# Native float32 second products for the first eight pairs, and a first-weights product as four side-by-side tiles that DMA spreads

## The chip, the cores and the metric

The kernel runs on one core of a Trainium2 chip. The metric is the device time of one execution in microseconds (us); lower is better. Engines work in parallel, each in its own program order: PE (matrix products; PEld is its weight loading), DVE, ACT and POOL (elementwise work), and SP, which here issues every DMA.

## The reference

```python
# x: (4, 12480, 128)   inducing: (32, 128)   w_in: (128, 2048)   w_out: (2048, 128)
def mab(q, kv):
    s = scale * (q @ kv.transpose(0, 2, 1))
    s = s - s.max(-1, keepdims=True)
    a = np.exp(s)
    a /= a.sum(-1, keepdims=True) + 1e-09
    return a @ kv
h = mab(I, x)                 # 32 induced points for each batch, over all 12480 tokens
y = mab(x, h)                 # each token attends to the 32 points
r = np.maximum(y @ w_in, 0.0)
out = (s * (r * r) + b) @ w_out
```

## The kernel before

The tokens of a batch form 26 blocks of 480 (`BLK`); four batches give 104 blocks. The 2048 hidden features form 16 chunks of 128, taken two at a time: 8 *pairs* for a block, 832 pairs in all, numbered `k`.

**The two products of a pair.** The kernel never forms `y`. It multiplies the induced points with `w_in` first (`w_unit`, tile `wst`), so that the first product of a pair is `wst` times the attention weights `a2t` of the block. Matmuls on `float32r` operands are the quick kind; on plain `float32` operands the same matmul leaves two records and takes longer. To keep accuracy with `float32r`, an operand is split in a rounded high part and the rest: `wst` holds the high part of the points' product in rows 0 to 63 and the low part in rows 64 to 127, `a2t` repeats its own high and low parts to match, and `w_out` is split in `w_hi` and `w_lo` (`split_w_out`). After the first product (`pair`, two matmuls, PSUM tile `h`, three buffers) ACT or DVE takes the relu `r`, ACT squares it in `float32r` (`square`, tile `g1`), DVE forms the exact square `g` (called the S step below, L831), and POOL or DVE subtracts the two for the rest `g2` (L845). The second product (`out_part`) is six matmuls: `w_lo` and `w_hi` on `g1`, `w_hi` on `g2`.

**Work beside the pairs.** For each batch there are, beside the pairs of the batch before: `scores` (seven groups of up to four blocks), `top`, `values` (seven groups, each with two halves of the keys' tile `xn`, L633), `points` (the induced points, `hT`), `w_unit` (four chunks of 512 features, L560, each with an ACT cast L562 and a DVE subtraction L564), and `attend` (seven groups, L681 and the DVE steps L687 to L712). `spread` sends an attend's high and low parts (tile `hl`, two buffers) to `a2t` (three buffers) by four SP DMAs for a block (L774). `scores`, `attend` and `values` use PE on tiles of 32 columns, four side by side.

**The opening.** Batch 0 has nothing to hide behind: its phase 1 runs first (`p1_unit`, `turn_x`), then `h_unit`, `h_out` (tile `hT`), four chunks of `w_unit`, `attend_first` (the first block alone, `a2t` by PE and ACT), and only then pairs. The weights arrive as 64-bit floats and `narrow` makes them `float32` by integer steps on DVE (L291 to L307), ACT and POOL (L312), chunk by chunk; `w_out`'s chunks are then split, and summed for the bias (`w_sum`, L329; `bias_unit`). `keep_warm` issues idle matmuls until the first `a2t` is there.

**What sets the order.** Class `Plan` is a planner that runs while the program is built. Each step names an engine, an expected duration, events to wait for and an urgency; the planner takes steps by expected start plus `WEIGHT` (0.0272 us) times urgency, lowest first, and so writes out a fixed order for every engine. Constants such as `FIRST`, `FIRST_FRONT`, `W_IN_U`, `W_OUT_U`, `SPREAD` are urgencies; `ATTEND_AT`, `W_AT` and others are block numbers at which work beside the pairs is placed. `front_work` strings the work beside a block into one chain. The planner also decides for each pair whether POOL or DVE does the subtraction (`kind`).

Of the kernel before, what the change touches and what calls it, by code (L numbers as in the profile page):

```python
# [19 lines left out]
P = 128  # L20
# [29 lines left out]
SPREAD = -50.0  # L50
FIRST_FRONT = -120.0
W_IN_U = -190.0
W_OUT_U = -100.0
W_URGENCY = (1.5, 20.0, 21.0, 22.0)

# [9 lines left out]
H_AT = 20  # L65
W_AT = (20, 21, 21, 21)
NEXT_AT = 23
# [76 lines left out]
def tile_attn_relu2(ctx: ExitStack, tc: tile.TileContext, xT, xN, indT, w_in, w_out, s_rep, b_rep, outT):  # L144
# [123 lines left out]
    def load_weight(gate, name, c):  # L268
        turn, free = ring("g1", 4)
        yield "SP", 0.05, free, *gate  # L270
        sl = slice(c * WC, (c + 1) * WC)
        src, dst = (w_in, w_in_sb) if name == "w_in" else (
            w_out.rearrange("p f d -> p (f d)"), w_out_raw.rearrange("p f d -> p (f d)")
        )
        raw = ew.tile([P, WC, 2], I32, name="g1", bufs=4)
        nc.sync.dma_start(out=raw.rearrange("p n w -> p (n w)"), in_=src[:, sl].bitcast(I32))
        raws[name, c] = raw, turn
        plan.events["raw", name, c] = landing(1.46)
        plan.spawn(narrow((name, c), dst[:, sl], ("raw", name, c)), W_IN_U if name == "w_in" else W_OUT_U)
        if name == "w_out":  # L280
            plan.spawn(split_w_out(c), W_OUT_U)


    def narrow(name, dst, *waits):
        raw, turn = raws.pop(name)
        hi, lo = raw[:, :, 1], raw[:, :, 0].bitcast(U32)
        e_turn, e_free = ring("g", 4)
        m_turn, m_free = ring("g2", 8)
        yield "DVE", 0.36, e_free, *waits
        e = ew.tile([P, WC], I32, name="g", bufs=4)  # L290
        nc.vector.tensor_scalar(  # L291
            out=e, in0=hi, scalar1=20, scalar2=0x7FF, op0=ALU.logical_shift_right, op1=ALU.bitwise_and
        )
        yield "DVE", 0.36, m_free
        m = ew.tile([P, WC], I32, name="g2", bufs=8)
        nc.vector.tensor_scalar(out=m, in0=hi, scalar1=0xFFFFF, scalar2=None, op0=ALU.bitwise_and)
        yield "DVE", 0.36
        nc.vector.tensor_scalar(out=e, in0=e, scalar1=896.0, scalar2=1151.0, op0=ALU.max, op1=ALU.min)
        yield "ACT", 0.5
        nc.scalar.activation(out=dst, in_=m, func=AF.Copy, scale=2.0**-20, bias=1.0)  # L300
        plan.set(("g2", m_turn))
        yield "ACT", 0.5
        nc.scalar.activation(out=e, in_=e, func=AF.Copy, scale=2.0**23, bias=-896 * 2.0**23)
        yield "DVE", 0.6
        nc.vector.scalar_tensor_tensor(out=dst, in0=lo, scalar=2.0**-52, in1=dst, op0=ALU.mult, op1=ALU.add)
        yield "DVE", 0.6
        nc.vector.scalar_tensor_tensor(  # L307
            out=e, in0=hi, scalar=-0x80000000, in1=e, op0=ALU.bitwise_and, op1=ALU.bitwise_or
        )
        plan.set(("g1", turn))  # L310
        yield "Pool", 1.4
        nc.gpsimd.tensor_tensor(out=dst, in0=dst, in1=e.bitcast(F32), op=ALU.mult)  # L312
        plan.set(("g", e_turn))
        plan.set(name)

    def split_w_out(c):
        raw = w_out_raw
        sl = slice(c * (WC // P), (c + 1) * (WC // P))
        yield "ACT", 0.6, ("w_out", c)
        nc.scalar.copy(out=w_hi[:, sl, :], in_=raw[:, sl, :])  # L320
        yield "Pool", 1.3
        nc.gpsimd.tensor_tensor(
            out=w_lo[:, sl, :], in0=raw[:, sl, :], in1=w_hi[:, sl, :].bitcast(F32), op=ALU.subtract
        )
        plan.set(("w_split", c))
        if c % 2:
            both = slice((c - 1) * (WC // P), (c + 1) * (WC // P))
            yield "DVE", 1.15, ("w_out", c - 1)
            nc.vector.reduce_sum(  # L329
                out=w_sum[:, c // 2, :], in_=raw[:, both, :].rearrange("p f d -> p d f"), axis=AX.X  # L330
            )
        plan.set(("w_sum", c))
# [217 lines left out]

    def w_unit(b, c, ps, *waits):
        d = st[b]
        lo = P // 2
        sl = slice(c * WC, (c + 1) * WC)
        yield "PE", 0.85, ("hT", b), ("w_in", c), *waits
        if c == 0:
            d["wst"] = wst_pool.tile([P, F], F32R, name="wst")
        wst = d["wst"]
        ps = ps()
        nc.tensor.matmul(ps, d["hT"], w_in_sb[:, sl], start=True, stop=True)  # L560
        yield "ACT", 0.6
        nc.scalar.copy(out=wst[:, sl], in_=ps)  # L562
        yield "DVE", 0.6
        nc.vector.tensor_sub(out=wst[lo:P, sl], in0=ps[lo:P, :], in1=wst[lo:P, sl].bitcast(F32))  # L564
        plan.set(("wst", b, c))

# [3 lines left out]
    def scores(b, g, ps, *waits):  # L570
# [40 lines left out]
    def values(b, g, ps, *waits):  # L611
# [10 lines left out]
        plan.set(("eT", "got", e_turn))  # L622
        nc.vector.transpose(out=eT[0:rows].rearrange("p n i -> p (n i)"), in_=e)
        for half in range(-(-TB // TH)):
            runs = range(half * TH, min(TB, (half + 1) * TH))
            yield "PE", 0.055 * len(runs) + 0.1, ("xn", b, g, half)
            if half == 0:
                ps = ps()
            xn, xn_turn = xn_tiles.pop((b, g, half))
            plan.set(xn_turn)  # L630
            for n in runs:
                c = n % (P // M)
                nc.tensor.matmul(  # L633
                    ps[M * c:M * (c + 1), 0:P], eT[0:rows, n], xn[0:rows, n - runs.start],
                    start=n < P // M, stop=n + P // M >= TB,
                )
        plan.set(("eT", e_turn))
# [35 lines left out]
    def attend(b, g, ps, *waits):  # L673
        nb = blocks_in(g)
        rows = M * nb
        yield "PE", 0.2 + 0.2 * nb, ("hT", b), ("x", b, g, 2), *waits
        ps = ps()
# [29 lines left out]
        yield dict(ACT=0.56, DVE=0.65), 0.0, *free  # L707
        hl = p2.tile([P, 2, BLK], F32R, name="hl")
        plan.set(("hl", "got", n))
# [9 lines left out]
    def attend_first(ps):  # L719
# [26 lines left out]
        yield dict(ACT=0.38, DVE=0.43), 0.0  # L746
        A = p2.tile([P, 2, BLK], F32R, name="hl")
        A = A.rearrange("p a t -> p (a t)")[0:T, 0:NQ * P].rearrange("p (n r s i) -> p n r s i", n=NQ, r=2, s=2)
# [17 lines left out]
    def spread(b, g, q):  # L766

        turn, free = ring_in_order("a2t", 3)
        yield "SP", 1.4, *free, ("hl", b, g)
        t = p2.tile([P, BLK], F32R, name="a2t", bufs=3)  # L770
# [21 lines left out]
    def pair(k):  # L792
# [28 lines left out]
        plan.set(("R", k))  # L821
        q["R"].append((n, plan.end))
        if len(q["R"]) == 1:
            plan.spawn(square(k - n), k + SQ, plan.end + LAT)
        yield "DVE", 1.07, S_U
        wait = max(0.0, pool_work[0] - plan.end)
        kind = "P" if wait < POOL_Q and next_free("g", 4) <= plan.start else "D"
        if kind == "P":
            g_turn, _ = ring("g", 4)
        g = hv if kind == "D" else ew.tile([P, 2, BLK], F32, name="g", bufs=4)  # L830
# [51 lines left out]
    def out_part(k, ops, us, weights, used):  # L882
# [6 lines left out]
        first = left == 2 * NPAIR  # L889
        left -= 1  # L890
        parts[blk_g] = left
# [49 lines left out]
    for b in range(B):  # L941
        at = b * NBLK
        units = [(ATTEND_AT[g - 1], attend, b, g) for g in range(1, NG)]
        if b + 1 < B:
            units += [(SCORES_AT[g], scores, b + 1, g) for g in range(NG)]
            units += [(VALUES_AT[g], values, b + 1, g) for g in range(NG)]
            units += [(TOP_AT, top, b + 1), (H_AT, points, b + 1), (NEXT_AT, attend, b + 1, 0)]
            units += [(W_AT[c], w_unit, b + 1, c) for c in range(F // WC)]
        rank = [scores, top, values, points, w_unit, attend]
# [23 lines left out]

    def w_work(c):
        t = hs[1 + c // 2]
        yield from w_unit(0, c, lambda: t[:, c % 2])
        if c % 2:
            plan.set(("h", 1 + c // 2))

# [39 lines left out]
    def after():  # L1019
        yield "SP", 0.05, *[("p1", 0, g) for g in range(NG)]  # L1020
        plan.spawn(h_unit(0, lambda: hs[2][:, 0]), FIRST)
        plan.spawn(h_out(0, lambda: hs[2][:, 1]), FIRST)
        for c in range(F // WC):
            plan.spawn(w_work(c), FIRST + W_URGENCY[c])
        plan.spawn(attend_first(lambda: bank[0]), FIRST)
# [48 lines left out]
```

## Time and profile before

| | |
|---|---|
| median of 3 runs | 1628.44 us (1628.23 to 1628.54) |
| profiled execution, time | 1628.27 us |
| profiled execution, span of the engines | 1626.2 us |
| PE busy | 1606.7 us, 99% |
| POOL busy | 1570.5 us, 97% |
| ACT busy | 1513.9 us, 93% |
| DVE busy | 1463.8 us, 90% |
| mean granted PE clock | 0.998 of full speed |

The span is the stretch from the first to the last instruction; 2.07 us of the profiled execution lie around it. Busy times are sums over each engine; matmul ends are modelled, so the starts of successive matmuls tell more than their durations. In a row of the timeline the columns are start (us from the span's start), time (us), engine, line, operation, tile written and tile read, count of merged instructions, and in brackets how long the engine had been idle and what released it. In a row of the groups, the number after the bar is the group's busy time, then the mean of one in ns, then idle time before them.

### The profile page before, as it was taken

To read this page: it belongs to the slowest core of one execution; us is meant where nothing else is said; L and a number is where in the kernel's file an instruction comes from. 1 tells how busy PE (TensorE), PEld (TensorE's weight loads), DVE (VectorE), ACT (ScalarE), POOL (GpSimd) and SP (SyncE) were. 2 spreads that over 40 slices of the span, in tenths; PEclk is the share of its full clock that TensorE was granted. 3 is DMA by queue.
4 is the path that set the end of the run, shared out by engine and by line. 5 is a ranking of instruction groups with operands and counts; after the bars stand their busy time and mean duration, and the time that the engine had idled before them with its cause. 6 is when DMAs were issued, how large, how long until landed. Compare 5 with 4: busy or idle time off the path is not lost.

```text
span 1626.2 us, 24652 instructions
## 1 busy us (share of the span) xinstructions
PE 1606.7 (99%) x8159; PEld 1300.1 (80%) x8159; DVE 1463.8 (90%) x1587; ACT 1513.9 (93%) x1771; POOL 1570.5 (97%) x715
## 2 busy tenths in 40 slices
PE   9799999999999999999999999999999999999998
PEld 6577878888887787888788787887878888888787
DVE  6999989989998998989899989989989889999897
ACT  7799999989999999899999999999999999999997
POOL 1699999999999999999999999999999999999998
PEclk9999999999999999999999999999999999999999
DMA  7132223311133222231122322322212112112100
GB/s 270 59 110 96 75 70 113 109 50 61 37 104 112 77 92 83 88 110 55 43 67 98 103 80 73 116 80 86 61 43 68 37 50 67 32 49 68 55 31 19
DMA packets 50909, 125.99 MB, mean 77 GB/s; under 512 B 10464, under 2 KB 36960, under 8 KB 50784
## 3 DMA queue, kind: packets, MB, share of 16 engines
q1 hardware_dynamic: 50784, 124.43, 23.9%
q8 instruction: 66, 1.08, 0.3%
q14 instruction: 59, 0.48, 0.1%
HBM read 73.52 MB, written 25.56 MB: 61 GB/s over the span
## 4 chain that ended last, share of the span: by engine, by line
PE 91%; POOL 3%; DVE 2%; ACT 2%; issue 2%; DMA 0%; POOLq 0%; DVEq 0%; ACTq 0%
PE x L893 63%; PE h L803 21%; POOL g L845 3%; PE x L633 1%; PE x L681 1%; PE x L590 1%; ACT r L818 1%; PE h L404 1%; PE x L560 1%; DVE g L831 1%; ACT g L868 1%; PE x L429 0%; PE x L458 0%; DVE w_sum L329 0%; DMA xt<-in_xT_dram 0%
## 5 line engine op out<-in xcount | busy, mean ns | idle before, releaser
L845 POOL TENSOR_TENSOR g<-g,g 128x960 fp32r<-128x960 f32 x696 | 1553.5, 2289 | 4.0 <-DVE g L831 2.9
L893 PE MATMUL x<-g,w_hi 128*128 128x480 f32 x3328 | 1058.6, 382 | 2.1 <-POOL g L845 2.1
L831 DVE SCALAR_TENSOR_TENSOR g<-h,r 128x960 f32<-128x960 f32 x696 | 784.7, 1148 | 67.1 <-ACT r L818 49.8
L868 ACT ACTIVATE g<-r 128x960 fp32r<-128x960 f32 (+1 forms) x807 | 802.8, 1029 | 18.2 <-DVE r L820 5.6
L893 PEld LDWEIGHTS x<-g,w_hi 128*128 128x128 f32 x3328 | 620.8, 188 | 126.4 <-POOL g L845 16.2
L818 ACT ACTIVATE r<-h 128x960 f32<-128x960 f32 x659 | 625.6, 968 | 53.5 <-PE h L803 42.5
L893 PE MATMUL x<-g,w_lo 128*128 128x480 f32 x1664 | 636.1, 382 | 6.5 <-ACT g L868 6.5
L803 PE MATMUL h<-a2t,wst 128*128 128x480 f32 x1664 | 506.0, 385 | 1.8 <-DVE g L831 1.0
L803 PEld LDWEIGHTS h<-a2t,wst 128*128 128x128 f32 x1664 | 305.8, 188 | 81.8 <-issue 23.9
L893 PEld LDWEIGHTS x<-g,w_lo 128*128 128x128 f32 x1664 | 313.1, 188 | 60.5 <-issue 11.4
L820 DVE TENSOR_SCALAR r<-h 128x960 f32<-128x960 f32 x173 | 199.2, 1152 | 18.9 <-PE h L803 15.5
L845 DVE TENSOR_TENSOR g<-h,g 128x960 fp32r<-128x960 f32 x136 | 156.7, 1152 | 7.8 <-ACT g L868 2.1
L831 DVE SCALAR_TENSOR_TENSOR h<-h,r 128x960 f32<-128x960 f32 x136 | 157.5, 1158 | 5.5 <-ACT r L818 4.8
L901 ACT ACTIVATE ob<-x,bias,s_sb 128x480 f32<-128x480 f32 x103 | 77.0, 747 | 12.5 <-PE x L893 11.7
L312 POOL TENSOR_TENSOR w_in_sb<-w_in_sb,g 128x512 f32<-128x512 f32 x4 | 5.4, 1342 | 28.7 <-DVE g L307 28.7
L681 PE MATMUL x<-xt,hT 128*32 128x480 f32 x208 | 28.3, 578 | 0.0
L633 PE MATMUL x<-xn,eT 128*32 128x128 f32 (+1 forms) x630 | 26.9, 279 | 0.0
L633 PEld LDWEIGHTS x<-xn,eT 128*32 128x32 f32 (+1 forms) x630 | 15.6, 108 | 14.1 <-issue 11.7
L687 DVE STREAM_TRANSPOSE x<-x 128x480 f32<-128x480 f32 (+1 forms) x28 | 19.4, 693 | 7.5 <-PE x L681 6.9
L712 DVE TENSOR_TENSOR hl<-x,hl 128x480 fp32r<-128x480 f32 (+1 forms) x28 | 18.4, 656 | 5.4 <-ACT hl L175 5.1
L696 DVE TENSOR_REDUCE x<-x 128x15 f32<-128x480 f32 (+1 forms) x28 | 18.5, 661 | 4.1 <-ACT x L694 3.7
L590 PE MATMUL x<-xt,ind_sb 128*32 128x480 f32 x156 | 21.2, 578 | 0.0
(150 smaller groups left out, 416.2 us busy)
## 6 DMA issues: line engine op xcount, KB each, us to landing
xt<-in_xT_dram SPq DMA_DIRECT2D x41, 960.0 KB, 4.9
out_dram<-ob SPq DMA_DIRECT2D x104, 240.0 KB, 2.0
a2t<-hl SPq DMA_DIRECT2D x412, 60.0 KB, 2.0
xn<-in_xN_dram SPq DMA_DIRECT2D x18, 512.0 KB, 3.6
xn<-in_xN_dram SPq DMA_DIRECT2D x18, 448.0 KB, 4.4
xt<-in_xT_dram SPq DMA_DIRECT2D x13, 480.0 KB, 3.8
r<-in_xT_dram SPq DMA_DIRECT2D x7, 480.0 KB, 9.2
g<-in_w_in_dram SPq DMA_DIRECT2D x4, 512.0 KB, 11.2
```

Of the source, the lines that this page charges most:

```text
L590: nc.tensor.matmul(ps[M * q:M * (q + 1), 0:BLK], ind_sb, xt[:, q], start=True, stop=True)
L633: nc.tensor.matmul(ps[M * c:M * (c + 1), 0:P], eT[0:rows, n], xn[0:rows, n - runs.start], start=n < P // M, stop=n + P // M >= TB,)
L681: nc.tensor.matmul(ps[M * q:M * (q + 1), 0:BLK], hT[:, 0:M], xt[:, q], start=True, stop=True)
L687: nc.vector.transpose(out=s, in_=s)
L803: nc.tensor.matmul(h[:, u, 0:BLK], wst[:, c * P:(c + 1) * P], A, start=True, stop=True)
L818: nc.scalar.activation(out=r, in_=hv, func=AF.Relu)
L820: nc.vector.tensor_scalar(out=r, in0=hv, scalar1=0.0, scalar2=None, op0=ALU.max)
L831: nc.vector.scalar_tensor_tensor(out=g, in0=hv, scalar=0.0, in1=r, op0=ALU.max, op1=ALU.mult)
L845: eng.tensor_tensor(out=g2, in0=g, in1=hi.bitcast(F32), op=ALU.subtract)
L868: nc.scalar.activation(out=q["g1_t"][:, sl, :], in_=q["r_t"][:, sl, :], func=AF.Square)
L893: nc.tensor.matmul(o, w, g, start=first and n == 0, stop=left == 0 and n == len(ops) - 1)
L901: nc.scalar.activation(out=ob, in_=o, func=AF.Identity, bias=bias, scale=s_sb)
```

## The change

1. For the first eight pairs (`k < NATIVE`), the second product is two plain `float32` matmuls of `w_out_raw` on the exact square `g`: no `square`, no subtraction, and no need of `w_hi` and `w_lo`. `split_w_out` and the sums get a late urgency (`SPLIT_U`, `W_SUM_U`) in place of -100.
2. `w_unit` is one step for a batch: four matmuls of 32 columns side by side into one bank, one cast and one subtraction for all (tile `hl`), and 16 SP DMAs (`spread_w`, four for a chunk) that write the high and low parts to the rows of `wst`.
3. The PE part of `values` is one step that waits for both halves of `xn`, where it was two steps.
4. The planner's durations for `narrow`, `w_sum`, `scores`, `attend` and `spread`, and the urgency `FIRST_FRONT`, have other values. `hl` grows to 2 x 512 columns.

```diff
-FIRST_FRONT = -120.0
+FIRST_FRONT = -60.0
+SPLIT_U = 5.0
+NATIVE = 8
+W_SUM_U = 6.0
-W_URGENCY = (1.5, 20.0, 21.0, 22.0)
+W_URGENCY = 1.5
-W_AT = (20, 21, 21, 21)
+W_AT = 21
...
-            plan.spawn(split_w_out(c), W_OUT_U)
+            plan.spawn(split_w_out(c), SPLIT_U)
...
-            yield "DVE", 1.15, ("w_out", c - 1)
+            yield "DVE", 1.98, ("w_out", c - 1), W_SUM_U - SPLIT_U
...
-    def w_unit(b, c, ps, *waits):
+    def w_unit(b, ps, *waits):
         d = st[b]
-        lo = P // 2
-        sl = slice(c * WC, (c + 1) * WC)
-        yield "PE", 0.85, ("hT", b), ("w_in", c), *waits
-        if c == 0:
-            d["wst"] = wst_pool.tile([P, F], F32R, name="wst")
-        wst = d["wst"]
-        ps = ps()
-        nc.tensor.matmul(ps, d["hT"], w_in_sb[:, sl], start=True, stop=True)
-        yield "ACT", 0.6
-        nc.scalar.copy(out=wst[:, sl], in_=ps)
-        yield "DVE", 0.6
-        nc.vector.tensor_sub(out=wst[lo:P, sl], in0=ps[lo:P, :], in1=wst[lo:P, sl].bitcast(F32))
-        plan.set(("wst", b, c))
+        nc_ = F // WC
+        yield "PE", 1.3, ("hT", b), *[("w_in", c) for c in range(nc_)], *waits
+        d["wst"] = wst_pool.tile([P, F], F32R, name="wst")
+        ps = ps()
+        for c in range(nc_):
+            nc.tensor.matmul(
+                ps[M * c:M * (c + 1), :], d["hT"][:, 0:M], w_in_sb[:, c * WC:(c + 1) * WC], start=True, stop=True
+            )
+        n, free = ring_in_order("hl", 2)
+        yield dict(ACT=0.59, DVE=0.7), 0.0, *free
+        hl = p2.tile([P, 2, WC], F32R, name="hl")
+        plan.set(("hl", "got", n))
+        copy(hl[:, 0], ps)
+        yield "DVE", 0.7
+        nc.vector.tensor_sub(out=hl[:, 1], in0=ps, in1=hl[:, 0].bitcast(F32))
+        left = list(range(nc_))
+        for c in range(nc_):
+            plan.spawn(spread_w(b, c, hl, n, left), SPREAD + c, plan.end + LAT)
+
+    def spread_w(b, c, hl, n, left):
+        yield "SP", 2.4
+        wst = st[b]["wst"]
+        for r in range(P // M):
+            nc.sync.dma_start(
+                out=wst[M * r:M * (r + 1), c * WC:(c + 1) * WC].bitcast(F32),
+                in_=hl[M * c:M * (c + 1), r * M // (P // 2)].bitcast(F32),
+            )
+        left.remove(c)
+        if not left:
+            plan.set(("hl", n))
+        plan.events["wst", b, c] = landing(0.8)
...
+        yield "PE", 1.25, *[("xn", b, g, half) for half in range(-(-TB // TH))]
+        ps = ps()
+        for n in range(TB):
+            c, half = n % (P // M), n // TH
+            nc.tensor.matmul(
+                ps[M * c:M * (c + 1), 0:P], eT[0:rows, n], xn_tiles[b, g, half][0][0:rows, n - half * TH],
+                start=n < P // M, stop=n + P // M >= TB,
+            )
...
+        native = k < NATIVE
...
-        q["R"].append((n, plan.end))
-        if len(q["R"]) == 1:
-            plan.spawn(square(k - n), k + SQ, plan.end + LAT)
-        yield "DVE", 1.07, S_U
+        if native:
+            g1_used(q, 2)
+            q["r_uses"] -= 1
+            kind = "N"
+            g_turn, g_free = ring("g", 4)
+            yield "DVE", 1.07, S_U, g_free
+        else:
...
+        if kind == "N":
+            ops = [(w_out_raw[:, 2 * pr + u, :], g[:, u, :]) for u in range(2)]
+            plan.spawn(out_part(k, ops, 1.6, "w_out", lambda: plan.set(("g", g_turn))), k + OUT, plan.end + LAT)
+            return
```

More of the change, by code (lines that the diff above doesn't have):

```diff
@@ L288, in narrow @@
         m_turn, m_free = ring("g2", 8)
-        yield "DVE", 0.36, e_free, *waits
+        yield "DVE", 0.45, e_free, *waits
         e = ew.tile([P, WC], I32, name="g", bufs=4)
@@ L293, in narrow @@
         )
-        yield "DVE", 0.36, m_free
+        yield "DVE", 0.45, m_free
         m = ew.tile([P, WC], I32, name="g2", bufs=8)
         nc.vector.tensor_scalar(out=m, in0=hi, scalar1=0xFFFFF, scalar2=None, op0=ALU.bitwise_and)
-        yield "DVE", 0.36
+        yield "DVE", 0.45
         nc.vector.tensor_scalar(out=e, in0=e, scalar1=896.0, scalar2=1151.0, op0=ALU.max, op1=ALU.min)
-        yield "ACT", 0.5
+        yield "ACT", 0.63
         nc.scalar.activation(out=dst, in_=m, func=AF.Copy, scale=2.0**-20, bias=1.0)
         plan.set(("g2", m_turn))
-        yield "ACT", 0.5
+        yield "ACT", 0.63
         nc.scalar.activation(out=e, in_=e, func=AF.Copy, scale=2.0**23, bias=-896 * 2.0**23)
-        yield "DVE", 0.6
+        yield "DVE", 0.72
         nc.vector.scalar_tensor_tensor(out=dst, in0=lo, scalar=2.0**-52, in1=dst, op0=ALU.mult, op1=ALU.add)
-        yield "DVE", 0.6
+        yield "DVE", 0.72
         nc.vector.scalar_tensor_tensor(
@@ L310, in narrow @@
         plan.set(("g1", turn))
-        yield "Pool", 1.4
+        yield "Pool", 1.3
         nc.gpsimd.tensor_tensor(out=dst, in0=dst, in1=e.bitcast(F32), op=ALU.mult)
@@ L549, in h_out @@
         plan.set(("hT", b))
-    def w_unit(b, c, ps, *waits):
+    def w_unit(b, ps, *waits):
         d = st[b]
-        lo = P // 2
-        sl = slice(c * WC, (c + 1) * WC)
-        yield "PE", 0.85, ("hT", b), ("w_in", c), *waits
-        if c == 0:
-            d["wst"] = wst_pool.tile([P, F], F32R, name="wst")
-        wst = d["wst"]
-        ps = ps()
-        nc.tensor.matmul(ps, d["hT"], w_in_sb[:, sl], start=True, stop=True)
-        yield "ACT", 0.6
-        nc.scalar.copy(out=wst[:, sl], in_=ps)
-        yield "DVE", 0.6
-        nc.vector.tensor_sub(out=wst[lo:P, sl], in0=ps[lo:P, :], in1=wst[lo:P, sl].bitcast(F32))
-        plan.set(("wst", b, c))
+        nc_ = F // WC
+        yield "PE", 1.3, ("hT", b), *[("w_in", c) for c in range(nc_)], *waits
+        d["wst"] = wst_pool.tile([P, F], F32R, name="wst")
+        ps = ps()
+        for c in range(nc_):
[24 more added lines that the diff above has]
+        plan.events["wst", b, c] = landing(0.8)
     def scores(b, g, ps, *waits):
@@ L585, in scores @@
         d = st[b]
-        yield "PE", 0.2 + 0.2 * nb, ("x", b, g, 1), *waits
+        yield "PE", 0.4 + 0.23 * nb, ("x", b, g, 1), *waits
         ps = ps()
@@ L623, in values @@
         nc.vector.transpose(out=eT[0:rows].rearrange("p n i -> p (n i)"), in_=e)
-        for half in range(-(-TB // TH)):
-            runs = range(half * TH, min(TB, (half + 1) * TH))
-            yield "PE", 0.055 * len(runs) + 0.1, ("xn", b, g, half)
-            if half == 0:
-                ps = ps()
[L629 to L636, printed above, removed]
+        yield "PE", 1.25, *[("xn", b, g, half) for half in range(-(-TB // TH))]
[6 more added lines that the diff above has]
+            )
+        for half in range(-(-TB // TH)):
+            plan.set(xn_tiles.pop((b, g, half))[1])
         plan.set(("eT", e_turn))
@@ L675, in attend @@
         rows = M * nb
-        yield "PE", 0.2 + 0.2 * nb, ("hT", b), ("x", b, g, 2), *waits
+        yield "PE", 0.4 + 0.23 * nb, ("hT", b), ("x", b, g, 2), *waits
         ps = ps()
@@ L707, in attend @@
         yield dict(ACT=0.56, DVE=0.65), 0.0, *free
-        hl = p2.tile([P, 2, BLK], F32R, name="hl")
+        hl = p2.tile([P, 2, WC], F32R, name="hl")[:, :, 0:BLK]
         plan.set(("hl", "got", n))
@@ L746, in attend_first @@
         yield dict(ACT=0.38, DVE=0.43), 0.0
-        A = p2.tile([P, 2, BLK], F32R, name="hl")
+        A = p2.tile([P, 2, WC], F32R, name="hl")
         A = A.rearrange("p a t -> p (a t)")[0:T, 0:NQ * P].rearrange("p (n r s i) -> p n r s i", n=NQ, r=2, s=2)
@@ L768, in spread @@
         turn, free = ring_in_order("a2t", 3)
-        yield "SP", 1.4, *free, ("hl", b, g)
+        yield "SP", 2.4, *free, ("hl", b, g)
         t = p2.tile([P, BLK], F32R, name="a2t", bufs=3)
@@ L821, in pair @@
         plan.set(("R", k))
-        q["R"].append((n, plan.end))
-        if len(q["R"]) == 1:
-            plan.spawn(square(k - n), k + SQ, plan.end + LAT)
-        yield "DVE", 1.07, S_U
[L826 to L829, printed above, removed]
+        if native:
[5 more added lines that the diff above has]
+        else:
+            q["R"].append((n, plan.end))
+            if len(q["R"]) == 1:
+                plan.spawn(square(k - n), k + SQ, plan.end + LAT)
+            yield "DVE", 1.07, S_U
+            wait = max(0.0, pool_work[0] - plan.end)
+            kind = "P" if wait < POOL_Q and next_free("g", 4) <= plan.start else "D"
+            if kind == "P":
+                g_turn, _ = ring("g", 4)
         g = hv if kind == "D" else ew.tile([P, 2, BLK], F32, name="g", bufs=4)
@@ L889, in out_part @@
         first = left == 2 * NPAIR
-        left -= 1
+        left -= 2 if weights == "w_out" else 1
         parts[blk_g] = left
@@ L947, in tile_attn_relu2 @@
             units += [(TOP_AT, top, b + 1), (H_AT, points, b + 1), (NEXT_AT, attend, b + 1, 0)]
-            units += [(W_AT[c], w_unit, b + 1, c) for c in range(F // WC)]
+            units.append((W_AT, w_unit, b + 1))
         rank = [scores, top, values, points, w_unit, attend]
@@ L972, in turn_work, with w_work @@
         yield from turn_x(g, h, lambda: hs[j % 2], ("turn", j - 2))
[L974 to L978, printed above, removed]
+    def w_work():
+        yield from w_unit(0, lambda: hs[1][:, 0])
+        plan.set(("h", 1))
+        plan.set(("h", 2))
     def opening():
@@ L1022, in after @@
         plan.spawn(h_out(0, lambda: hs[2][:, 1]), FIRST)
-        for c in range(F // WC):
-            plan.spawn(w_work(c), FIRST + W_URGENCY[c])
+        plan.spawn(w_work(), FIRST + W_URGENCY)
         plan.spawn(attend_first(lambda: bank[0]), FIRST)
```

## The prediction

> **What bounds the kernel now.** I read the page's busy times first, then a table of stretches, to see whether one engine is the bound everywhere or only on average.
>
> ```profile
> PE 1606.7 (99%) x8159; PEld 1300.1 (80%) x8159; DVE 1463.8 (90%) x1587; ACT 1513.9 (93%) x1771; POOL 1570.5 (97%) x715
> ```
>
> ```profile
> core 0: us, PE busy (x) PEld busy (x) DVE busy (x) ACT busy (x) POOL busy (x), PEclk, DMA share, GB/s
> 52.00:60.00 8.00, 1.61 (x10) 1.05 (x6) 7.41 (x13) 5.66 (x8) 2.67 (x2) 0.89 0.36 123
> ...
> 100.00:400.00 300.00, 299.76 (x1555) 242.02 (x1554) 273.82 (x293) 281.74 (x332) 299.82 (x136) 1.00 0.27 87
> ...
> 1200.00:1600.00 400.00, 398.35 (x1830) 330.90 (x1829) 367.13 (x372) 386.73 (x434) 399.66 (x180) 1.00 0.16 49
> ```
>
> From 100 to 1600 us PE has no room: 299.76 of 300 us busy, at full clock. What leaves PE there shortens the run one for one, as long as the others follow. POOL is as full, but it shares its subtraction with DVE, which is busy 91% there. Between 52 and 60 us it is different: PE stands for 6.4 of 8 us, and the clock drops. So the steady part is priced in PE time, the opening in PE's gaps.
>
> **Steady part, `w_unit`.** I looked for what one chunk costs PE, from the starts of its neighbours:
>
> ```profile
> 391.36 1.02 PE L560 MATMUL x<-w_in_sb,hT 128*128 128x512 f32 x2
> 391.79 0.19 PEld L803 LDWEIGHTS h<-a2t,wst 128*128 128x128 f32 x1 [0.24 <-PE x L893]
> 391.82 1.00 PE L803 MATMUL h<-a2t,wst 128*128 128x480 f32 x2
> 392.66 0.60 PE L893 MATMUL x<-g,w_hi 128*128 128x480 f32 x2
> ```
>
> ```profile
> 84.90 0.38 PE L893 MATMUL x<-g,w_lo 128*128 128x480 f32 x1
> 85.12 0.38 PE L893 MATMUL x<-g,w_hi 128*128 128x480 f32 x1
> 85.43 1.01 PE L590 MATMUL x<-xt,ind_sb 128*32 128x480 f32 x8
> 86.37 0.71 PE L803 MATMUL h<-a2t,wst 128*128 128x480 f32 x2
> 86.92 0.60 PE L893 MATMUL x<-g,w_hi 128*128 128x480 f32 x2
> ```
>
> Ordinary matmuls start 0.21 to 0.22 us apart, on average 0.217. From 391.36 to 392.66 lie 1.30 us; the two L803 in them take 0.43, so a chunk costs 0.87 us, four cost 3.48. The new form is like `scores`: four 32-column tiles. From 85.12 to 86.92 lie 1.80 us, less 0.217 and 0.433 for three ordinary matmuls: 1.15 us, of which 0.94 is the group itself (85.43 to 86.37). At 512 columns that is 0.94 x 512/480 + 0.21 = 1.21 us. Saving for a batch 2.27, for batches 1 to 3 **6.8 us**. The ends: 1.00 us without any switching cost (7.4 saved) and 3.48 if the tiles did not run side by side (0 saved); `scores` has the same form, so I take 1.21. ACT loses three of four casts and DVE three of four subtractions, both of which run beside PE: nothing.
>
> **Steady part, `values`.**
>
> ```profile
> 297.38 0.38 PE L893 MATMUL x<-g,w_lo 128*128 128x480 f32 x1
> 297.59 0.37 PE L893 MATMUL x<-g,w_hi 128*128 128x480 f32 x1
> 297.90 0.64 PE L633 MATMUL x<-xn,eT 128*32 128x128 f32 x16
> 298.47 0.70 PE L803 MATMUL h<-a2t,wst 128*128 128x480 f32 x2
> 299.10 0.64 PE L633 MATMUL x<-xn,eT 128*32 128x128 f32 x14
> 299.67 0.71 PE L803 MATMUL h<-a2t,wst 128*128 128x480 f32 x2
> ```
>
> Two ordinary matmuls stand between the halves and take 0.63 us (298.47 to 299.10) where they need 0.43: going out of the tiled form and into it again costs 0.20 us. Joined, that goes, once in each of 3 batches x 7 groups = 21: **4.2 us**. If the halves of some groups already touch it is less, down to 0. The one step waits for both `xn` loads, and keeps the first buffer some 1.2 us longer (0.57 + 0.63); both are fetched two blocks ahead, some 30 us (1570 us after the opening / 104 blocks is 15 each), so nothing waits.
>
> **Steady part, the 16 DMAs.** `spread_w` goes on SP, past the `a2t` spreads:
>
> ```profile
> L774 SPq DMA_DIRECT2D a2t<-hl x412: 507/582/1692, 60.5 to 1583.1; - x138
> DMA to landing us min/median/max: 1.9/2.0/5.6
> ```
>
> ```profile
> SPq L774 <- PE h L803: 42.4, 23, 10.7
> ```
>
> 16 issues take 16 x 0.582 = 9.3 us and land 2.0 us later. `wst` is wanted five blocks (some 75 us) after `W_AT`. An `a2t` spread behind them comes 9.3 us late, but spreads waited 42.4 us for L803 to give back one of three `a2t` buffers, so they run about two blocks ahead. `hl` is held for those 11 us too; the next attend but one needs it. I take 0 and bound it in a rival.
>
> **Opening.** The rows below carry this part.
>
> ```profile
> 44.22 3.68 PE L560 MATMUL h<-w_in_sb,hT 128*128 128x512 f32 x8
> 46.36 1.08 ACT L562 CAST wst<-h 128x512 fp32r<-128x512 f32 x2
> 50.73 0.56 ACT L175 CAST a2t<-x 128x480 fp32r<-128x480 f32 x1 [0.40 <-PE x L757]
> 51.10 1.01 PE L681 MATMUL x<-xt,hT 128*32 128x480 f32 x8
> 52.04 1.57 PE L803 MATMUL h<-a2t,wst 128*128 128x480 f32 x6
> 54.51 0.70 DVE L687 STREAM_TRANSPOSE x<-x 128x480 f32<-128x480 f32 x1
> 58.20 1.79 ACT L868 ACTIVATE g<-r 128x1920 fp32r<-128x1920 f32 x1
> 59.19 0.70 DVE L705 STREAM_TRANSPOSE x<-x 128x480 f32<-128x480 f32 x1
> 60.14 0.74 PE L893 MATMUL x<-g,w_lo 128*128 128x480 f32 x1 [6.53 <-ACT g L868]
> 60.67 0.60 PE L893 MATMUL x<-g,w_hi 128*128 128x480 f32 x1
> 61.07 0.60 PE L893 MATMUL x<-g,w_lo 128*128 128x480 f32 x1
> ```
>
> ```profile
> 53.50:58.50 5.00, 0.11 (x1) 0.00 (x0) 4.44 (x9) 4.16 (x7) 1.51 (x2) 0.98 0.45 175
> 58.50:65.30 6.80, 5.16 (x13) 4.38 (x14) 6.38 (x8) 4.48 (x5) 3.45 (x3) 0.52 0.19 47
> ```
>
> ```profile
> L803 PE MATMUL h<-a2t,wst 128*128 128x480 f32 x47 | 14.0, 390 | 1.1 <-DVE g L831 1.0
> L831 DVE SCALAR_TENSOR_TENSOR g<-h,r 128x960 f32<-128x960 f32 x18 | 20.2, 1150 | 2.9 <-ACT r L818 1.8 <-POOL g L845 1.1
> L818 ACT ACTIVATE r<-h 128x960 f32<-128x960 f32 x20 | 18.9, 974 | 2.5 <-PE h L803 2.4
> L322 POOL TENSOR_TENSOR w_lo<-wst,w_hi 128x512 fp32r<-128x512 f32 x4 | 5.5, 1365 | 3.3 <-ACT w_hi L320 3.3
> ```
>
> *Before*, PE loses after its first pair (52.04): 6.5 us until the square, 1.1 before L803, 0.2 small, and the half clock. The clock was halved after 5 us of idling and stayed so to 65.3; until about 65.1 twelve matmuls start 0.40 us apart (60.67 to 61.07) instead of 0.217, a loss of 2.3 us. Together 10.1 us.
>
> *When the first pair starts after.* The tiles need 1.0 us after 44.2 (PE is behind `attend_first`), one cast of 0.6 and one subtraction of 0.7 follow: about 47.3. Four DMAs issue in 2.3 us, the last issue 1.75 us after the first and 2.0 to landing: chunk 0 at about 51.1, chunk 1 (pairs 2 and 3) 53.4, chunk 2 55.7, chunk 3 58.1. A landing of 1.9 to 5.6 us puts chunk 0 between 51.0 and 54.7. The other way, `a2t`, ends near 51 as before, perhaps 0.5 earlier with three fewer subtractions on DVE. Then the attend of group 0 (1 us) is ahead of the first pair on PE. So the first pair starts at 51.8, hidden behind attend: **-0.2 us** (range -0.7 to +2.9).
>
> *Native pairs on PE.* A plain 512-column matmul starts its passes 0.43 us apart (391.36 to 391.79), so a pass of 480 takes 0.40, two matmuls of two passes 1.60 us. Six `float32r` matmuls took 1.30. Eight pairs x 0.30: **+2.4 us**.
>
> *PE's gaps after.* A native pair waits for relu (0.97) and S (1.15), no square. Relu of pair 0 ends near 53.4, and DVE is then in the attend chain (54.51 to 59.89 before, 52.3 on now that `w_sum` is late). The chain leaves DVE free once, while ACT takes the exponential, about 54.4; I put S of pair 0 there, behind a `narrow` step of 0.4: it ends at 56.0. PE idles 52.7 to 53.6 and 54.0 to 56.2. The attend chain goes on to about 59.3, S of pair 1 ends at 60.5, and PE idles 2.4 us after native pair 0. From then a pair takes PE 1.60 + 0.43 and DVE 1.15, and PE is the bound; I allow 1 us of stumbles for `narrow`'s last chunk and `w_sum`. Sum 0.9 + 2.2 + 2.4 + 1.0 = 6.5, no half clock. Against 10.1: **-3.6 us**. The four splits now lie beside native pairs, where POOL has no subtraction to do; if that cover failed, PE would wait at pair 8 for at most their POOL parts, 5.5 us.
>
> **Sum:** -6.8 - 4.2 - 0.2 + 2.4 - 3.6 = -12.4; 1628.3 of the profiled execution (0.17 us below the median) gives **1616.0 us**.
>
> **The rivals.**
>
> *No stall in the opening.* S of pair 0 goes ahead of the attend chain: only the wait for relu and S stays (1.9 us), and 1 us of stumbles. Instead of 6.5, 2.9: 1612.4 us. For it: the chain's urgency falls from -120 to -60, a start advantage of 1.6 instead of 3.3 us. Against: -60 still beats S's -1.3.
>
> *A long stall.* S of pair 0 comes behind the whole chain: PE stands from 52.7 to 59.1 less one pair's first product, 6.0 us, then runs at half clock as before (2.3 to 3.4 us), and 1 us. That is about 10, all of the opening's gain: 1619.4 us.
>
> *The half clock at short gaps.* The trace has a halving after 5 us of idling, none after less. Between 52.7 and 56.2 PE would be idle for 3.1 of 3.5 us. If that suffices, 2.3 us are lost as before: 1618.3 us. The Trainium skill, TensorE: Matmul & The Clock Gate, Part 1, has the gate close after an idle window of about 3.4 us that runs freely. By that rule my two gaps stay just under it, and any slip of S by a microsecond would cross it, where the row's 5 us would still allow it; the trace here shows no gap between the two.
>
> *POOL bounds the rest.* If the full POOL (299.82 of 300), not PE, set the pace, the 11 us taken off PE would turn into idling: 1628.3 - 1.4 = 1626.9 us. Against: DVE, 9% idle, can take more subtractions.
>
> *Slower: SP.* If an `a2t` spread queued behind the 16 DMAs is wanted before they are through, PE stands in each of three batches. With half of 9.3 us uncovered and 2.3 for the clock: 3 x 7.0 = 20.9, 1636.8 us. It decides where the stall with its clock passes (12.4 + 3.3)/3 = 5.2 us a batch, a lead of spreads under about 6 us. Against: the lead of about 30 us read above.
>
> **Chances.** Forecast 0.40; no stall 0.18; half clock 0.12; long stall 0.14; POOL 0.08; SP 0.08. A change of 0.2% (3.3 us) is about what measurement can tell from none, so the POOL case counts as the same: faster 0.84, same 0.08, slower 0.08. The range leaves out SP and most of POOL, and below takes the no-stall case with 4 us for an earlier first pair and stumbles that do not come: 1608 to 1625.
>
> **What would show it.** L560 as eight 32-column records, about 1.2 us of PE a batch; L633 in one run of 30; from 100 us on PE still over 99.5% busy. In the opening: first L803 near 51.8, first native matmul near 56, block 0's output near 76, no stretch of low clock. Wrong would be: PE gaps in the steady part (POOL, or SP at the batch borders), a first pair held by `wst`'s landing, or a clock that is halved longer than before.

## The result: slower, and POOL has become the bound

| | before | after |
|---|---|---|
| median | 1628.34 us (1627.59 to 1628.54) | 1640.57 us (1639.56 to 1641.69) |
| profiled execution, span | 1626.2 us | 1637.8 us |
| subtractions on POOL / on DVE / native pairs | 696 / 136 / 0 | 699 / 125 / 8 |

After against before: ratio 1.0078, 95% interval 1.0065 to 1.0091. The prediction was 1616.0 us, faster than before; the kernel became slower, so the result lies outside its range (1608 to 1625) and on the other side of the kernel before.

The stretches of the kernel after, to set beside those of before (columns: stretch, length, then busy time and count of PE, PEld, DVE, ACT, POOL, granted clock, DMA share, GB/s):

```profile
80.00:100.00 20.00, 20.00 (x100) 15.88 (x93) 18.71 (x20) 19.00 (x23) 20.00 (x10) 1.00 0.28 91
100.00:400.00 300.00, 296.79 (x1550) 239.42 (x1550) 269.15 (x286) 277.39 (x326) 300.00 (x136) 1.00 0.27 88
400.00:800.00 400.00, 394.92 (x2000) 318.03 (x1999) 356.70 (x380) 369.26 (x431) 400.00 (x181) 1.00 0.26 84
800.00:1200.00 400.00, 395.32 (x2005) 318.73 (x2004) 358.31 (x381) 374.10 (x438) 400.00 (x180) 1.00 0.26 84
1200.00:1600.00 400.00, 397.75 (x1812) 325.70 (x1812) 364.37 (x372) 381.51 (x430) 400.00 (x181) 1.00 0.16 49
```

POOL is busy 1500.00 of 1500 us from 100 on. PE, which idled 0.24 us between 100 and 400 before, now idles 3.2 there, and 15.2 from 100 to 1600 (2.4 before). The slices of a tenth on the page still show 9 for both engines; only the hundredths tell which one waits.

POOL's group before and after, one row of each page, then the waits of DVE for POOL and of PE for DVE, each time before first, after second (waited for: us in total, times, longest):

```profile
L845 POOL TENSOR_TENSOR g<-g,g 128x960 fp32r<-128x960 f32 x696 | 1553.5, 2289 | 4.0 <-DVE g L831 2.9
```

```profile
L878 POOL TENSOR_TENSOR g<-g,g 128x960 fp32r<-128x960 f32 x699 | 1558.8, 2533 | 13.9 <-DVE g L860 13.9
```

```profile
DVE g L831 <- POOL g L845: 11.7, 18, 1.1
```

```profile
DVE g L860 <- POOL g L878: 61.3, 105, 1.1
```

```profile
PE h L803 <- DVE g L831: 1.0, 1, 1.0
```

```profile
PE h L824 <- DVE g L860: 7.2, 12, 2.9
```

The S step writes a `g` that POOL frees (four buffers). It waited 11.7 us for POOL before and 61.3 us after, and PE's waits for S grew from 1.0 to 7.2 us (2.9 of them one gap in the opening): POOL holds DVE, and DVE holds PE. All the idle time charged to POOL's subtractions, 13.9 us, lies ahead of the first one: from then on POOL runs without a gap. The mean of 2533 ns is not the price of one subtraction: 699 of them would be 1770 us, more than the group was busy, so the records overlap. 1558.8 / 699 = 2.23 us is the price, and before it was 1553.5 / 696 = 2.23 too.

The timeline of POOL after, its start and its end:

```profile
74.52 35.72 POOL L878 TENSOR_TENSOR g<-g,g 128x960 fp32r<-128x960 f32 x16 [13.89 <-DVE g L860]
...
1599.32 33.96 POOL L878 TENSOR_TENSOR g<-g,g 128x960 fp32r<-128x960 f32 x15
```

POOL's chain alone gives the span: 74.52 + 699 x 2.23 + 4.5 us behind its last subtraction (1633.28 to 1637.8) = 1637.8. In the kernel before the unbroken run began earlier and had four fewer:

```profile
63.09 2.25 POOL L845 TENSOR_TENSOR g<-g,g 128x960 fp32r<-128x960 f32 x1
65.28 1.33 POOL L322 TENSOR_TENSOR w_lo<-wst,w_hi 128x512 fp32r<-128x512 f32 x1
66.56 44.65 POOL L845 TENSOR_TENSOR g<-g,g 128x960 fp32r<-128x960 f32 x20
```

66.56 + 695 x 2.23 + 4.5 = 1621 us, 5.3 us inside the measured 1626.2. So before, PE held the time with POOL some 5 us behind it (e5 below tests this). After, POOL starts 8.0 us later and does four more in its run, 8.9 us, and passes PE: 8.0 + 8.9 - 5.3 = 11.6 us, which is the whole difference of the spans.

Why more, when eight pairs need no subtraction at all? The planner chooses POOL or DVE for each pair by *expected* times. It books 2.17 us for a POOL subtraction, which takes 2.23: some 42 us too little over 699. As long as POOL's booked backlog is under a limit (`POOL_Q`) and a `g` buffer is free, POOL gets the next one, so on paper POOL is kept full for as long as the plan lasts: count times booked duration is 1516.8 us here, and 1520.9, 1520.2 and 1521.0 in e1, e9 and e10 below, which change the booked duration alone. In the kernel before, PE's durations were partly too short as well: it booked 1.0 us for a `scores` group of four blocks, which the prediction's rows put at 1.15. The change made the durations of `scores` and `attend` longer (1.0 to 1.32 us for four blocks), and left POOL's. On paper PE became slower, and there was room for more subtractions on POOL.

### The profile page after: what moved, and what is told of

The parts are those of the page before. It is cut to its first block, busy times and chain, and to the rows that moved or that the text cites. A ratio compares the mean times of both kernels' runs of the same rounds, so it can differ in the third digit from the quotient of the medians.

```text
span 1637.8 us, 24676 instructions
## 1 busy us (share of the span) xinstructions
PE 1606.7 (98%) x8147; PEld 1288.9 (79%) x8147; DVE 1454.3 (89%) x1569; ACT 1500.6 (92%) x1755; POOL 1575.8 (96%) x718
## 5 line engine op out<-in xcount | busy, mean ns | idle before, releaser
L878 POOL TENSOR_TENSOR g<-g,g 128x960 fp32r<-128x960 f32 x699 | 1558.8, 2533 | 13.9 <-DVE g L860 13.9
L926 PE MATMUL x<-g,w_hi 128*128 128x480 f32 x3296 | 1046.5, 382 | 5.1 <-POOL g L878 4.6
L860 DVE SCALAR_TENSOR_TENSOR g<-h,r 128x960 f32<-128x960 f32 x707 | 801.8, 1149 | 116.2 <-POOL g L878 61.3
L901 ACT ACTIVATE g<-r 128x960 fp32r<-128x960 f32 x808 | 797.8, 1020 | 40.1 <-DVE r L842 25.0
L926 PEld LDWEIGHTS x<-g,w_hi 128*128 128x128 f32 x3296 | 612.4, 188 | 131.5 <-POOL g L878 27.3
L926 PE MATMUL x<-g,w_lo 128*128 128x480 f32 x1648 | 626.3, 380 | 0.0
L842 DVE TENSOR_SCALAR r<-h 128x960 f32<-128x960 f32 x179 | 205.5, 1149 | 16.5 <-PE h L824 15.1
L878 DVE TENSOR_TENSOR g<-h,g 128x960 fp32r<-128x960 f32 x125 | 143.8, 1150 | 6.7 <-ACT g L901 1.4
L860 DVE SCALAR_TENSOR_TENSOR h<-h,r 128x960 f32<-128x960 f32 x125 | 144.6, 1157 | 2.6 <-ACT r L840 1.9
L702 PE MATMUL x<-xt,hT 128*32 128x480 f32 x208 | 29.1, 594 | 0.0
```

The source lines that it names most:

```text
L702: nc.tensor.matmul(ps[M * q:M * (q + 1), 0:BLK], hT[:, 0:M], xt[:, q], start=True, stop=True)
L842: nc.vector.tensor_scalar(out=r, in0=hv, scalar1=0.0, scalar2=None, op0=ALU.max)
L860: nc.vector.scalar_tensor_tensor(out=g, in0=hv, scalar=0.0, in1=r, op0=ALU.max, op1=ALU.mult)
L878: eng.tensor_tensor(out=g2, in0=g, in1=hi.bitcast(F32), op=ALU.subtract)
L901: nc.scalar.activation(out=q["g1_t"][:, sl, :], in_=q["r_t"][:, sl, :], func=AF.Square)
L926: nc.tensor.matmul(o, w, g, start=first and n == 0, stop=left == 0 and n == len(ops) - 1)
```

## The experiments

My theory after the result was this chain of POOL: *start of its run of subtractions + count x 2.23 + 4.5*, the count being set by the planner's durations. The 2.23 and the 4.5 come from the kernel after; the runs below test them. The rival was that a new part (16 DMAs a batch, the held `hl` buffer, the native pairs) stops PE.

**e1: after, with POOL's duration at 2.23.**

```diff
-        yield ("Pool", 2.17, ("Q", k), free2) if kind == "P" else ...
+        yield ("Pool", 2.23, ("Q", k), free2) if kind == "P" else ...
-            pool_work[0] = max(pool_work[0], plan.end) + 2.17
+            pool_work[0] = max(pool_work[0], plan.end) + 2.23
```

> The kernel after, with the planner's duration of a POOL subtraction raised from 2.17 to 2.23 us, so that it hands POOL 682 subtractions in place of 699 (counted in the program). Theory (POOL's own chain sets the end: start of its first subtraction + count x 2.23 us + 4.5 us behind the last): POOL would be through at a span of 74.5 + 682 x 2.23 + 4.5 = 1600 us, so PE is the bound again and the time is that of my prediction with the better opening, about 1612 us (1608 to 1618). Rival (the 16 DMAs for a batch, the held hl buffer or another new part stops PE): the count doesn't matter, about 1640 us.

Measured 1608.9 us (1608.2 to 1609.46), ratio to before 0.9885 (0.987 to 0.990). The stretches of e1, the waits of DVE for POOL, and POOL's group:

```profile
100.00:400.00 300.00, 300.00 (x1578) 244.94 (x1577) 276.02 (x295) 284.17 (x336) 300.00 (x136) 1.00 0.27 88
400.00:800.00 400.00, 399.95 (x2041) 327.02 (x2040) 365.78 (x394) 381.22 (x444) 396.96 (x179) 1.00 0.26 84
...
1200.00:1600.00 400.00, 399.86 (x1843) 335.55 (x1842) 370.49 (x369) 385.80 (x433) 397.79 (x179) 1.00 0.15 48
```

```profile
DVE g L860 <- POOL g L878: 3.0, 4, 1.3
```

```profile
L878 POOL TENSOR_TENSOR g<-g,g 128x960 fp32r<-128x960 f32 x682 | 1522.3, 2334 | 19.2 <-DVE g L860 17.2 <-PE h L824 0.8 <-ACT hl L179 0.6
```

PE is full again, POOL has gaps (19.2 us idle, 5 of them after the start), and S waits 3.0 us for it. With every new part in place the loss is gone, so none of them is what stops PE. This version beats both kernels: it is 18.6 us under the 1627.49 that the kernel before took beside it.

**e2: before, with only the two PE durations changed** (`scores` first, `attend` second; `nb` is the number of blocks in the group).

```diff
-        yield "PE", 0.2 + 0.2 * nb, ("x", b, g, 1), *waits
+        yield "PE", 0.4 + 0.23 * nb, ("x", b, g, 1), *waits
-        yield "PE", 0.2 + 0.2 * nb, ("hT", b), ("x", b, g, 2), *waits
+        yield "PE", 0.4 + 0.23 * nb, ("hT", b), ("x", b, g, 2), *waits
```

> The kernel before, with only the planner's PE durations of scores and attend changed (0.2 + 0.2 nb to 0.4 + 0.23 nb); no instruction is added or removed, but the planner now gives POOL 705 subtractions in place of 696. Theory: POOL's chain ends later, 66.6 + 704 x 2.23 + 4.5 = 1641 us of span, so about 1643 us, slower than before by 15. Rival (the new parts themselves cost the time): no change, 1628 us.

Measured 1642.21 us, ratio 1.009 (1.0075 to 1.0105).

```profile
L845 POOL TENSOR_TENSOR g<-g,g 128x960 fp32r<-128x960 f32 x705 | 1571.9, 2304 | 0.0
```

```profile
66.27 29.02 POOL L845 TENSOR_TENSOR g<-g,g 128x960 fp32r<-128x960 f32 x13
```

66.27 + 704 x 2.23 + 4.5 = 1640.7, measured span 1640.4. Two numbers that issue nothing make the kernel before 15 us slower, more than the whole change did.

**e3: after, with the two old PE durations.** The edit of e2 the other way.

> The kernel after, with the old planner durations of scores and attend put back: 693 subtractions for POOL. Theory: 74.5 + 693 x 2.23 + 4.5 = 1624.4 us of span, about 1626 us, POOL still the bound. Rival (new parts): 1640 us.

Measured 1626.46 us, ratio 0.9995 (0.9985 to 1.0004). Span 1624.1, POOL's chain 74.50 + 693 x 2.23 + 4.5 = 1624.4. POOL is still the bound, only nearer.

**e4: after, with the old `w_unit`** (four full-width chunks, no DMAs).

> The kernel after with the old w_unit (four full-width chunks, no DMAs, no hl buffer): 703 subtractions for POOL. Theory: 74 + 703 x 2.23 + 4.5 = 1646 us of span, about 1648 us, slower than after. Rival (the 16 DMAs a batch or the held buffer stop PE): the loss goes, about 1625 us.

Measured 1648.57 us, ratio 1.0126 (1.0109 to 1.0143). Span 1647.0, chain 75.40 + 703 x 2.23 + 4.5 = 1647.6. Taking the new DMAs out does not undo the loss; the plan, now with more PE time in it, hands POOL four more, and it gets worse. By itself this does not rule the SP rival out, since POOL is the bound here whatever the DMAs do. e1 does: there all the DMAs are in place and PE is full.

**e5: before, with POOL's duration at 2.23.**

> The kernel before with the planner's POOL duration at 2.23 us: 680 subtractions for POOL in place of 696, nothing else. POOL would be through at a span of 66.5 + 679 x 2.23 + 4.5 = 1585 us. Theory A (before, PE and POOL were both full and either alone would have held the time): PE still needs its 1626 us of span, so no change, 1627 us, and POOL idles some 40 us. Theory B (POOL alone was the bound of before, PE only looked full): the time falls towards 1600 us.

Measured 1625.27 us, ratio 0.9985 (0.9975 to 0.9994).

```profile
L845 POOL TENSOR_TENSOR g<-g,g 128x960 fp32r<-128x960 f32 x680 | 1520.3, 2280 | 34.0 <-DVE g L831 20.4 <-ACT g L868 11.3 <-PE h L803 1.3
```

POOL idles 34 us and the time falls by 2.9 us; the interval lies just under 1, so 1 to 4 us of before's time were POOL's, and not the 28 that the second theory asked for. So PE was the bound of before, as I read it, with POOL close behind it. Giving POOL room is worth little without the PE time that the new parts take away.

**e6, e7, e8: e1 with one part undone.** With PE as the bound, these price my terms: `NATIVE = 0`; the old `w_unit`; the old two-step `values`.

> The kernel after with the POOL duration at 2.23 us and NATIVE = 0: the first block goes through square and subtraction again; 688 subtractions for POOL, its chain over at about 1600 us of span, so PE is the bound. This prices the native pairs in the opening against 1608.9 us. My prediction's terms for native pairs and gaps (+2.4 - 3.6) give +1.2, 1610 us; if the native pairs carry the whole opening (block 0 out 6 us earlier than before), about 1615 us.

> The kernel after with the POOL duration at 2.23 us and the old w_unit: 686 subtractions, POOL through at about 1611 us of span. My term for w_unit is 6.8 us over three batches, and with PE the bound the time is 1608.9 + 6.8 = 1616 us, and up to 3 more for a longer gap in the opening. If the 16 DMAs a batch cost something, less: 1609 to 1613 us.

> The kernel after with the POOL duration at 2.23 us and the old two-step values: 680 subtractions, POOL through at about 1597 us of span. My term is 21 x 0.20 = 4.2 us: 1613 us. If the joined step gains nothing (or makes other work wait), 1609 us or less.

| part undone | median | worth against e1 | my term |
|---|---|---|---|
| native pairs (e6) | 1610.2 | 1.3 | 3.6 - 2.4 = 1.2 |
| `w_unit` (e7) | 1617.0 | 8.1 | 6.8 |
| `values` (e8) | 1615.15 | 6.2 | 4.2 |

e6's runs go from 1608.34 to 1610.77, so 1.3 is hardly told from nothing. e8 came out 2 us over what I had expected of it. The kernel before took 1627.49 us beside e1 and 1628.18 beside e6, e7 and e8; with each version set against its own before, the three worths are 0.6, 7.4 and 5.6. Block 0's output starts at 77.50 us in e1, 77.46 in e7 and 79.70 in e8. From there to the end of the span the profiled executions need 1528.9, 1537.2 and 1534.3 us: 8.3 us for `w_unit` and 5.4 for `values`; the rest of e8's 6.2 lies in the opening, whose timing moves by about 2 us between the profiled executions.

The PE rows that show both parts: `w_unit` of the kernel after, then `values` of e8 (two steps) and of the kernel after (one step).

```profile
387.90 0.38 PE L926 MATMUL x<-g,w_hi 128*128 128x480 f32 x1
388.21 1.07 PE L564 MATMUL x<-w_in_sb,hT 128*32 128x512 f32 x8
389.20 0.70 PE L926 MATMUL x<-g,w_hi 128*128 128x480 f32 x2
389.75 0.60 PE L824 MATMUL h<-a2t,wst 128*128 128x480 f32 x2
```

```profile
266.54 0.64 PE L657 MATMUL x<-xn,eT 128*32 128x128 f32 x16
267.12 0.48 PE L929 MATMUL x<-g,w_lo 128*128 128x480 f32 x1
267.44 0.38 PE L929 MATMUL x<-g,w_hi 128*128 128x480 f32 x1
267.66 0.38 PE L929 MATMUL x<-g,w_lo 128*128 128x480 f32 x1
267.88 0.37 PE L929 MATMUL x<-g,w_hi 128*128 128x480 f32 x1
268.18 0.64 PE L657 MATMUL x<-xn,eT 128*32 128x128 f32 x14
268.75 0.70 PE L929 MATMUL x<-g,w_hi 128*128 128x480 f32 x2
```

```profile
266.49 0.82 PE L926 MATMUL x<-g,w_hi 128*128 128x480 f32 x3
267.24 1.07 PE L652 MATMUL x<-xn,eT 128*32 128x128 f32 x30
268.25 0.70 PE L824 MATMUL h<-a2t,wst 128*128 128x480 f32 x2
268.79 0.38 PE L926 MATMUL x<-g,w_lo 128*128 128x480 f32 x1
```

`w_unit`: 387.90 to 389.75 is 1.85 us, less 0.65 for three ordinary matmuls: 1.20 us, where I had 1.21. `values`: in e8 the two halves and the four ordinary matmuls between them take 2.21 us (266.54 to 268.75), less 0.87 for the four: 1.34 us. The joined group takes 1.01 us (267.24 to 268.25). That is 0.33 us a group, 0.13 beside the 0.20 of switching: 21 x 0.33 = 6.9 us at most. The rows give 3 x (3.48 - 1.20) = 6.8 us for `w_unit`; what lies above that (0.6 to 1.5 us) they do not explain.

**e9 and e10: the count, finer.** After with POOL's duration at 2.20 and at 2.26.

> The kernel after with the POOL duration at 2.20 us: 691 subtractions, half way between after (699) and e1 (682). Theory: time = larger of PE's need (1608.9 us, e1) and POOL's chain; 74.3 + 691 x 2.23 + 4.5 = 1619.7 us of span, so about 1621.5 us. If the gain of e1 came from another order of the work and not from the count, anything between 1609 and 1640.

> The kernel after with the POOL duration at 2.26 us: 673 subtractions, POOL through at 74.3 + 673 x 2.23 + 4.5 = 1580 us of span. Theory: PE holds the time at that of e1, 1609 us (1608 to 1612): fewer subtractions on POOL bring nothing more, and DVE still has room for the 9 more.

e9: 1623.31 us, ratio 0.9973 (0.9963 to 0.9983), 1.8 us over what I expected; its POOL run began at 75.47 us where I had put 74.3, which is 1.2 of it. e10: 1610.06, ratio 0.989 (0.9875 to 0.9904). Nine subtractions more than in e1 cost 14 us, nine fewer change nothing that can be told. That is a larger of two, not a slope, and it is what the chain gives.

**e11: after, with `NATIVE = 0`** and POOL's duration as it was.

> The kernel after with NATIVE = 0 and the POOL duration as it is (2.17): 705 subtractions, the first some 12 us earlier than after. Theory: 62 + 705 x 2.23 + 4.5 = 1639 us of span, 1640 us, the same as after: the native pairs start POOL later and take six subtractions off it, and the two cancel. If the native pairs were the cause of the loss: about 1627 us or less.

Measured 1638.9 us, ratio 1.0068 (1.0051 to 1.0085). Taking the native pairs out starts POOL 11 us earlier and gives it six more subtractions (13 us): the loss stays.

All profiled executions against the chain (the start of POOL's run is read from each trace, and the chain's end is what it would be if POOL never paused; a single subtraction ahead of the run is left out of the count in the third column):

| kernel | subtractions on POOL | run starts, count | chain's end | span | bound |
|---|---|---|---|---|---|
| before | 696 | 66.56, 695 | 1620.9 | 1626.2 | PE |
| after | 699 | 74.52, 699 | 1637.8 | 1637.8 | POOL |
| e1 | 682 | 74.23, 682 | 1599.6 | 1606.4 | PE |
| e2 | 705 | 66.27, 704 | 1640.7 | 1640.4 | POOL |
| e3 | 693 | 74.50, 693 | 1624.4 | 1624.1 | POOL |
| e4 | 703 | 75.40, 703 | 1647.6 | 1647.0 | POOL |
| e5 | 680 | 66.69, 679 | 1585.4 | 1623.3 | PE |
| e6 | 688 | 62.82, 687 | 1599.3 | 1606.5 | PE |
| e7 | 686 | 73.95, 686 | 1608.2 | 1614.7 | PE |
| e8 | 680 | 76.43, 680 | 1597.3 | 1614.0 | PE |
| e9 | 691 | 75.47, 691 | 1620.9 | 1621.3 | POOL |
| e10 | 673 | 75.86, 673 | 1581.2 | 1607.9 | PE |
| e11 | 705 | 63.30, 704 | 1637.7 | 1637.2 | POOL |

Wherever POOL never pauses, its chain gives the span to 0.6 us (in the kernel after by construction, in the five others as a test). Wherever the chain ends well before the span, POOL has gaps and PE is full: from 100 to 1600 us PE is busy at least 1497.6 us there, and POOL at most 1496.0.

## Why the prediction was wrong, step by step

**The step that failed** is in the first part: "POOL is as full, but it shares its subtraction with DVE". It does share it, but not at run time. The split is written into the program by the planner, by durations that the change alters. The durations are listed as part of the change, and the sum has no term for them: I priced them at nothing. e2 prices two of them in the kernel before, +14.7 us, and e3 in the kernel after, about 14 us. For the same reason "DVE, 9% idle, can take more subtractions", which I held against the POOL rival, was no defence: DVE takes only those that the plan gives it. The condition "as long as the others follow" was right, and POOL was the engine that could not. The prediction's own table had the sign: POOL was the fuller of the two in both long stretches that it shows, 299.82 us against PE's 299.76, and 399.66 against 398.35.

**The POOL rival** had the engine and the wrong size. It let POOL's work stand still and only the gain disappear (1626.9 us). It left out two things: POOL has nothing to do until the ninth pair, so its chain starts 8 us later; and the planner could give it more. I had even used the first, POOL free beside the native pairs, as cover for the splits, without asking what an engine without slack loses by starting late. The chain could have been worked out from rows I had: first subtraction, 1553.5 / 696, and the end. The count after the change stands in no trace of before; it is fixed when the program is built, and from e1 on I counted it there ahead of each run. 699 in place of 696 - 8 = 688 was worth 11 x 2.23 = 24.5 us.

**The steady terms were right in kind and somewhat low**: `w_unit` 7.4 to 8.3 for 6.8, `values` 5.4 to 6.2 for 4.2. They are PE time, and e1 shows them paid out once PE is the bound: with POOL's duration at 2.23 in both, before (e5) lies 2.9 us and after (e1) 18.6 us under the kernel before, so the change is worth 15.7 us there, where my sum had 12.4.

**The 16 DMAs** cost nothing that can be seen, as I took it. The measured time lies near the 1636.8 us of the SP rival by chance: in e1 the DMAs are all there and PE is busy 300.00 of 300 us.

**The opening.** The PE timeline of the kernel after:

```profile
50.53 0.54 PE L778 MATMUL x<-identr,hl 120*128 120x120 f32 x4 [2.67 <-DVE hl L773]
...
51.55 1.83 PE L702 MATMUL x<-xt,hT 128*32 128x480 f32 x8
53.30 2.18 PE L824 MATMUL h<-a2t,wst 128*128 128x480 f32 x6
58.35 1.17 PE L824 MATMUL h<-a2t,wst 128*128 128x480 f32 x2 [2.88 <-DVE g L860]
59.32 2.83 PE L926 MATMUL x<-g,wst 128*128 128x480 f32 x4
...
62.45 1.77 PE L926 MATMUL x<-g,wst 128*128 128x480 f32 x4
63.69 0.98 PE L824 MATMUL h<-a2t,wst 128*128 128x480 f32 x2
64.50 1.77 PE L926 MATMUL x<-g,wst 128*128 128x480 f32 x4
```

S of pair 0 stood inside the attend chain, in ACT's exponential, as I had placed it, but the first pair began at 53.30, not 51.8, and the first native product at 59.3, not 56.2. Half of the first delay is the clock: the attend group ahead of the pair (L702) takes 1.75 us (51.55 to 53.30) in place of 0.94. S came late because two `narrow` steps on DVE (0.68 and 0.69 us) stood ahead of it, where I had one of 0.4. Then PE ran without a break: a native pair takes 2.05 us (62.45 to 64.50), where I had 2.03, and the second long gap that I had allowed between pairs 0 and 1 did not come. (The 391.79 that I read as the start of a second pass is a weight load's row; the 0.43 us also follow from 0.87 for a chunk of two passes.) Block 0's output starts at 77.79 us; I had said near 76. Before, it started at 83.47, but these 5.7 us are no measure of the gain: without the native pairs (e6) it starts at 81.38, 3.9 us later than in e1, and the time is only 1.3 us longer. The rival of the half clock at short gaps was right in kind: the clock was halved after the gap that it named, and once more after a gap ahead of the first pair that I had not looked at.

## What to carry to other kernels

In a kernel whose order and division of work are written out ahead by expected durations, a changed duration is a change of the program: correct those of all engines that share work together, and price the new division, not only the instructions. Where two engines are both close to 99% busy, as here, work out each one's own chain (start + count x time of one + tail); the later end is the time, and what is taken off the other engine is worth nothing until it is shorter too. An engine without slack pays in full for a later start.

## What was not expected of the hardware

The granted clock of PE after, in short stretches:

```profile
47.80:50.40 2.60, 0.06 (x1) 0.00 (x0) 2.56 (x5) 0.37 (x1) 1.97 (x3) 1.00 0.40 101
50.40:52.40 2.00, 1.87 (x14) 0.84 (x14) 2.00 (x3) 1.08 (x2) 1.25 (x2) 0.70 0.39 98
52.40:53.40 1.00, 1.00 (x9) 0.10 (x1) 1.00 (x1) 0.00 (x0) 1.00 (x1) 0.50 0.91 158
53.40:55.40 2.00, 2.00 (x6) 1.44 (x6) 1.97 (x5) 1.53 (x3) 0.15 (x1) 0.69 0.77 253
55.40:58.30 2.90, 0.08 (x1) 0.00 (x0) 2.90 (x6) 2.30 (x4) 1.26 (x1) 0.96 1.06 374
58.30:59.30 1.00, 0.94 (x2) 0.83 (x3) 0.93 (x4) 0.98 (x2) 0.00 (x0) 0.50 0.97 384
59.30:60.30 1.00, 1.00 (x3) 0.51 (x2) 0.93 (x3) 0.74 (x1) 0.94 (x1) 0.50 0.99 340
60.30:62.30 2.00, 2.00 (x6) 0.85 (x5) 2.00 (x3) 0.79 (x2) 0.33 (x1) 0.71 0.22 50
```

A gap of 2.67 us was enough for a half clock, and the half clock came 0.7 us after PE was at work again (50.53): 0.70 over 2 us is 1.2 us at half, from 51.2 on, then 1.0, then 0.69 over 2 us another 1.2, 3.4 us in all. The gap of 2.88 us (up to 58.35) brought a second one, which began just before its end: 0.96 over 2.9 us is 0.2 us at half, from 58.1 on, then 1.0, 1.0 and 1.2, 3.4 us again. Before, a gap of 6.53 us had brought 6.8 us of it. The Trainium skill, TensorE: Matmul & The Clock Gate, Part 1, speaks of an idle window of about 3.4 us that runs freely. The lengths agree with such windows (one after each gap here, two before), and the two halvings here begin 6.9 us apart, about two windows. But both gaps were shorter than a window, so on that reading a window that was partly busy counted as idle; how busy it may be, no run here tests.
